# Scores of two slots in one visit, x^T between the double slots, PSUM laid out anew: threshold attention and an exact-Gelu MLP on one core

## The chip, the core and the metric

The kernel runs on one core of a Trainium2 chip. Its time is the device time of one execution in microseconds. Five engines work side by side and wait for each other by semaphores: TensorE (PE in the profile, its weight loads PEld), VectorE (DVE), ScalarE (ACT), GpSimd (POOL) and SyncE (SP, here only a queue of DMA issues). Each takes its instructions in the order in which the program was built.

## What is computed

```python
q, k, v: (8, 8, 576, 64)          # batch, heads, sequence, head dimension
scores = (q @ k^T) / 8
thresh = max(scores, -1) - tau
scores = where(scores >= thresh, scores, -1e9)
attn = exp(scores - max(scores));  attn /= sum(attn) + 1e-9
x = (attn @ v) laid out as (8*576, 512)
h = x @ w_in                       # (512, 2048)
out = (0.5 * h * (1 + erf(h / sqrt(2)))) @ w_out
```

All of it is float32. On TensorE a float32 matmul of this kernel is two instructions.

## The kernel before

**Pairs and slots.** Two heads of a batch make a pair; there are 32 pairs (`NP`), four to a batch. The 576 rows of a pair's scores are four chunks of 128 rows per head and a tail of 64 rows; the two tails share one tile. So a pair has five slots (`SLOTS`): chunks 0 to 3, each with both heads (`e` = 0, 1), and the tail (`NC` = 4). The first four pairs (`EARLY`) run in another way, with transposes on TensorE; the change leaves them nearly alone. From the fifth pair on the loop at line 1060 treats one slot after the other.

**A slot.** `scores` (L394) multiplies 64 rows of q^T with k^T; the two heads use the two halves of the array's rows at the same time, in two matmuls of 288 columns each. Each head has a PSUM tile of two banks (tag `sc`, two buffers). `softmax_head` (L406) takes for each head the maximum on VectorE (L415), the threshold on GpSimd (L416), and the exponential on ScalarE (L418). `softmax_tail` (L421) reads the scores again on VectorE, multiplies the exponentials with (score >= threshold) and sums them (L434). After it the `sc` tile is free. `turn_p` (L488) transposes 32x32 blocks on VectorE into `turned_p` (chunks) or `pd_tail` (tail). `regroup` (L504) issues DMAs on SP that bring the turned blocks into `pT`, of which there is one per head; so they wait until x^T of the pair before has been computed. `weigh_v` (L522) multiplies v with `pT` to x^T, in two column spans of 320 and 256, each in a PSUM bank of the ring `mm`; ScalarE copies them to `xall` (L547). `divisors` (L466) sends the sums through DRAM, and `divide` (L556) scales x on GpSimd. `turn_qk` (L375) and `scale_q` (L371) prepare the next pair's q and k, which `load_steps` (L251) has fetched through GpSimd's queue.

**The MLP between the slots.** `fill` (L637) issues MLP matmuls into TensorE's order, so many after each slot as its share of a goal (`GOAL`, L1042) and of the five slots (`PARTS`, L1053) asks for. `block_steps` (L602) walks a block of 256 tokens: 16 groups of four matmuls of 256 columns into `hT` (one bank takes two groups, eight matmuls), then 2 x 16 matmuls of 512 columns into `o_ps`. The Gelu of an hT tile is an instruction of ScalarE (L586); `gelus(left)` (L573) issues those that wait until only `left` are left. They are issued after a slot's exponentials (L1075, with 0 left) or by `fill` when a further tile is complete and more than `lag` wait (`lag` = 2, L1133). Gelu and Exp need different tables of ScalarE, so a load stands ahead of each change; `table` (L596) brings the Exp table back. Eight blocks (`PLAIN`) are done so during attention; the other ten come after it in `last_blocks` (L973), with fewer products by a Strassen scheme.

**PSUM.** One pool `ps` (L80) for the whole kernel: ring `mm` of four banks (hT, o_ps, x^T, transposes) and ring `sc` of two tiles of two banks, eight banks in all.

**Order before in a pair**, on TensorE: scores of chunk 0, fill, chunk 1, fill, chunk 2, x^T of the pair before (`WEIGH` = 2), a short fill, chunk 3, fill, tail, fill.

Of the kernel before, what the change touches and what calls it, by code (L numbers as in the profile page):

```python
# [18 lines left out]
def kernel(  # L19
# [28 lines left out]
    nc = tc.nc  # L48
# [30 lines left out]
    dram = ctx.enter_context(tc.tile_pool(name="dram", bufs=1, space=bass.MemoryType.DRAM))  # L79
    ps = ctx.enter_context(tc.tile_pool(name="ps", bufs=4, space=PSUM))  # L80

# [62 lines left out]
    nc.vector.memset(zeros, 0.0)  # L144
    idle = ps.tile([P, 2 * P], FP32, tag="mm", name="idle")
    for _ in range(3):
# [154 lines left out]
    def turn_qk_early(p):  # L301
# [12 lines left out]
        for name in "qk":  # L314
            t = s[name]
            tr = ps.tile([P, NC, P], FP32, tag="mm", name="tr")
            for c in range(NC):
                for e in range(2):
                    nc.tensor.matmul(tr[e * D:(e + 1) * D, c, :], lhsT=t[:, e, c, :], rhs=ident, start=True, stop=True)
            src = tr.rearrange("p c s -> p (c s)")  # L320
            if name == "q":
                nc.scalar.activation(qT, src, AF.Copy, bias=0.0, scale=q_scale)
            else:
                copy(kT[:, TAIL:S], src)
        tr = ps.tile([P, NC, P], FP32, tag="mm", name="tr")
        for j, name in enumerate("qk"):
# [12 lines left out]
    def turn_p_early(p, i):  # L339
# [11 lines left out]
        for e in range(n):  # L351
            tr = ps.tile([P, NC, P], FP32, tag="mm", name="tr")
            for c in range(NC):
                turn(tr[:, c, :], e * (S + TAIL) + c * P)
            if i < NC:
                nc.scalar.copy(s["pT"][e][:, 0:NC, i * P:(i + 1) * P], tr)  # L356
# [4 lines left out]
        tails = s["pT"][0][:, NC, :]  # L361
        tr = ps.tile([P, NC, P], FP32, tag="mm", name="tr")
        turn(tr[:, 0, :], MAIN if i < NC else S - P)
# [29 lines left out]

    def scores(p, i):  # L394
        s = st[p]
        n = 1 if i == NC else 2
        sc = s["sc", i] = [ps.tile([P, 2, 512], FP32, tag="sc", name="sc", bufs=2) for _ in range(n)]
        for h in range(2):
            for e in range(n):
                rows = slice(0, P) if i == NC else slice(e * D, (e + 1) * D)  # L400
                lhsT = s["q_tail"] if i == NC else s["qT"][rows, i * P:(i + 1) * P]
                at = h * HALF + (TAIL if p < EARLY and e == 0 else 0)
                nc.tensor.matmul(  # L403
                    sc[e][:, h, 0:HALF], lhsT=lhsT, rhs=s["kT"][rows, at:at + HALF], start=True, stop=True)

    def softmax_head(p, i):  # L406
# [6 lines left out]
        for e in range(n):  # L413
            sc = s["sc", i][e][:, :, 0:HALF]
            nc.vector.tensor_reduce(nmx[:, e:e + 1], sc, axis=AXIS.XY, op=ALU.max, negate=True)  # L415
            nc.gpsimd.tensor_scalar(  # L416
                thr[:, e:e + 1], nmx[:, e:e + 1], -1.0, tau_eff, op0=ALU.mult, op1=ALU.subtract)
            nc.scalar.activation(  # L418
                w[:, e * S:(e + 1) * S].rearrange("p (h s) -> p h s", h=2), sc, AF.Exp, bias=nmx[:, e:e + 1], scale=1.0)

    def softmax_tail(p, i):  # L421
# [10 lines left out]
        for e in range(n):  # L432
            row = w[:, e * S:(e + 1) * S].rearrange("p (h s) -> p h s", h=2)
            nc.vector.scalar_tensor_tensor(  # L434
                row, sc[e][:, :, 0:HALF], thr[:, e:e + 1], row, op0=ALU.is_ge, op1=ALU.mult, accum_out=den[e])
        if p < EARLY:
# [8 lines left out]
    def divide_early(p, lo, hi):  # L445
# [3 lines left out]
        b, hp = divmod(p, HP)  # L449
        tr = ps.tile([P, 512], FP32, tag="mm", name="tr")  # L450
        for i in range(lo // P, -(-hi // P)):
# [69 lines left out]

    def weigh_v(p, lo, hi):  # L522


        b, hp = divmod(p, HP)
        s = st[p]
        xT = ps.tile([P, 512], FP32, tag="mm", name="xT")
        for c in range(KR):
            for e in range(2):
                f = slice(e * D, (e + 1) * D)  # L530
                to = xT[f, 0:hi - lo]
                if p < EARLY:
                    rhs = s["pT"][0 if c == NC else e][:, c, lo:hi]
                else:
                    to = to.rearrange("p (g s) -> p g s", s=2 * Q)
                    rhs = by_64(s["pT"][e])[:, lo // (2 * Q):hi // (2 * Q), c, :]
                nc.tensor.matmul(  # L537
                    to, lhsT=s["v"][:, e, c, :], rhs=rhs, start=(c == 0), stop=(c == KR - 1))
        for n, o, at, size in in_blocks(b, lo, hi):
            if n not in x_blk:  # L540
# [61 lines left out]
    def block_steps(n):  # L602
# [3 lines left out]
        for j in range(N_DF):  # L606
            if j % 2 == 0:
                hT = None
            for c in range(N_DM):
                yield NS_IN, (j * P // PIECE + 1) * N_DM  # L610
                if hT is None:
                    hT = ps.tile([P, 2, TOK], FP32, tag="mm", name="hT")
                nc.tensor.matmul(hT[:, j % 2, :], lhsT=w_in_sb[c][:, j * P:(j + 1) * P], rhs=x_blk[n][:, c, :],  # L613
                                 start=(c == 0), stop=(c == N_DM - 1))
            if j % 2:
                late.append((g, j, hT))
                gelus(lag[0])
        x_free.append(x_at.pop(n))
        for m in range(TOK // P):
            for j in range(N_DF):  # L620
# [5 lines left out]
                if j == 0:  # L626
                    o = ps.tile([P, 512], FP32, tag="mm", name="o_ps")
                nc.tensor.matmul(o[:, 0:d_model], lhsT=g[j][:, m * P:(m + 1) * P], rhs=w_out_sb[j],  # L628
                                 start=(j == 0), stop=(j == N_DF - 1))
            o_sb = op.tile([P, d_model], FP32, tag="o_sb", name="o_sb")  # L630
            nc.scalar.copy(o_sb, o[:, 0:d_model])
            row = n * TOK + m * P
            nc.sync.dma_start(out[row:row + P, :], o_sb)

    mlp = {"n": 0, "steps": None, "next": None, "debt": 0.0, "layer": 0}

    def fill(ns, tokens):  # L637

        mlp["debt"] += ns
        while True:  # L640
# [7 lines left out]
            took, need = mlp["next"]  # L648
            if mlp["debt"] <= 0 or need > converted[0]:
                break  # L650
# [153 lines left out]
    def bank(tag, n):  # L804
        if tag == "sc":
            return ps.tile([P, 2, 512], FP32, tag="sc", name="bank", bufs=2)[:, 0, 0:n]
        return ps.tile([P, 512], FP32, tag="mm", name="bank")[:, 0:n]

# [221 lines left out]

    parts = [(range(2), HP), (range(2, SLOTS), HP)] + [(range(SLOTS), 1)] * (NP - HP)
    slots = []
# [19 lines left out]

    PARTS = 1.3, 1.3, 0.2, 1.3, 0.9  # L1053

# [5 lines left out]
    for n in range(len(slots) + WEIGH + 1):  # L1060
        p, i = slots[n] if n < len(slots) else divmod(n, SLOTS)
        early = p < EARLY
        last = slots[n - 1] if 0 < n <= len(slots) else None
        if p < NP:
            scores(p, i)
            softmax_head(p, i)
            add_low_bits()
# [4 lines left out]
        elif n == len(slots):  # L1072
            early_end.close()
            weights_first()
        gelus(0)  # L1075
        if n == BATCH:
            gelus_held()
        table()
        for args in due:
            weigh_v(*args)  # L1080
            divide_early(*args)
        due = []
        if p > EARLY and i == WEIGH:
            for lo, hi in (0, WIDE), (WIDE, S):
                weigh_v(p - 1, lo, hi)
            if p == NP:
                divide(p - 1)
        owed += (goal(n) - goal(n - 1)) * BLK_NS * (PARTS[i] if not early and p < NP else 1.0)
        if early:
# [7 lines left out]
        if p < NP:  # L1097
            softmax_tail(p, i)
        if p < NP and not early:
            turn_p(p, i)  # L1100
        if p < NP and not early:
            if i == 2:
                regroup(p, 1)
            if i > 2:
                regroup(p, i)
            if i == NC:
                divisors(p)
# [10 lines left out]
        if n == BATCH:  # L1118
            for t in pd_tail + [turned_p[:, e, h, :, :] for e in range(2) for h in range(2)]:
                nc.gpsimd.memset(t[:, NB:4 * KR, :], 0.0)  # L1120
        if EARLY < p < NP and i == DIVIDE:
            divide(p - 1)
        if p >= HP and i == 1 and p + 2 < NP:
            loads = load_steps(p + 2)
        if p >= HP:
            next(loads, None)
        if p >= HP and i == 1 and p + 1 < NP or p == HP - 1 and i == 2:
            scale_q(p + 1)
        if p >= HP - 1 and i == 2 and p + 1 < NP:
            turn_qk(p + 1)  # L1130
        convert(0 if n == 0 else 1200 if n < 3 else 2200 if n < BATCH - 1 else 1e9)
        if not early:
            lag[0] = 2 if p < NP else 0  # L1133
            if n != BATCH:
                fill(owed, tokens)
                owed = 0.0
# [7 lines left out]
        elif n == BATCH + 1:  # L1144
            tokens = S
        elif p > EARLY and i == DIVIDE and p % HP == 0 or p == NP and i == WEIGH:
            tokens = p // HP * S
            leaving += [n for n in AWAY if n in x_blk and (n + 1) * TOK <= tokens]
        elif leaving and i < 2:
            put_away(leaving.pop(0))  # L1150
    fill(1e12, B * S)
    late_end.close()
    last_blocks()

# [31 lines left out]
```

## Time and profile before

| | us |
|---|---|
| median of 3 runs (1350.87 to 1352.63) | 1350.93 |
| the profiled execution | 1353.51 |
| its span, first to last instruction | 1351.4 |
| mean of an exponential (L418), 288 of them | 0.738 |
| mean of a maximum (L415) | 0.750 |
| mean of a threshold step (L434) | 0.816 |
| mean of a chunk's turn (L498) | 1.378 |
| mean of a Gelu (L586), 56 of them | 0.597 |
| one table load of ScalarE, 55 at L586 and 55 at L599 | 1.283 |

How to read it: the page gives each engine's busy time, then the span in 40 slices, then the chain of work that ended last, then groups of instructions of one line, with the mean of one and the idle time just before them. The early pairs take the first 190 us or so, attention with MLP between runs to about 860 us, and the last ten blocks take the rest. In a stretch of the attention stage the maxima, thresholds, turns and exponentials of one pair (some 25 us) are all there, and the busy shares say how near each engine is to being the bound.

### The profile page before, as it was taken

How to read it: one execution, taken by the hardware profiler on the slowest of the kernel's cores; microseconds unless marked ns; L12 is line 12 of the kernel's file. 1: busy time of each engine (PE TensorE's matmuls, PEld its weight loads, DVE VectorE, ACT ScalarE, POOL GpSimd, SP SyncE). 2: the span in 40 equal slices, each digit the busy share in tenths (PEclk: the TensorE clock that was granted, in tenths of full speed). 3: DMA queues.
4: the chain of work that ended last, by engine and by line, in shares of the span. 5: the costliest groups of instructions: out<-in, count | busy, mean ns of one | idle time of the engine just before them, and what ended most of it. 6: DMA issues, size and time to landing. Idle time of an engine off the chain costs nothing.

```text
span 1351.4 us, 19821 instructions
## 1 busy us (share of the span) xinstructions
PE 1323.0 (98%) x6282; PEld 893.8 (66%) x6282; DVE 1048.1 (78%) x1997; ACT 605.0 (45%) x1027; POOL 659.0 (49%) x1097
## 2 busy tenths in 40 slices
PE   8799899999999999999999999999999999999998
PEld 6476557467467557557557557568787787877877
DVE  6987677788888888888888888874758698385765
ACT  7876527548547538537638636413201112211120
POOL 5785354555555554554554551144363513635530
PEclk9899999999999999999999999999999999999999
DMA  8642276677777787687687777500000041000003
GB/s 268 187 151 52 58 164 156 146 162 185 155 180 182 161 193 178 160 207 172 153 208 180 155 179 152 117 9 0 1 0 1 14 112 32 0 1 0 1 0 78
DMA packets 209781, 152.39 MB, mean 113 GB/s; under 512 B 113360, under 2 KB 193088, under 8 KB 209680
## 3 DMA queue, kind: packets, MB, share of 16 engines
q1 hardware_dynamic: 188224, 112.53, 37.5%
q0 software_dynamic: 21024, 38.32, 9.9%
q8 instruction: 51, 0.84, 0.3%
q14 instruction: 50, 0.41, 0.1%
q10 hardware_dynamic: 432, 0.30, 0.1%
HBM read 55.97 MB, written 12.52 MB: 51 GB/s over the span
## 4 chain that ended last, share of the span: by engine, by line
PE 93%; DVE 3%; ACT 3%; DMA 1%; issue 1%; SPq 0%; POOL 0%; DVEq 0%; ACTq 0%; POOLq 0%
PE bank L801 34%; PE o_ps L628 17%; PE hT L613 16%; PE sc L403 14%; PE xT L537 11%; ACT p L418 1%; DMA x<-xall 1%; DVE nmx L415 1%; DVE p L434 1%; PE tr L349 1%; ACT pT L356 1%; DVE power L212 0%; ACT power L202 0%; DVE power L210 0%; PE tr L456 0%
## 5 line engine op out<-in xcount | busy, mean ns | idle before, releaser
L418 ACT ACTIVATE p<-sc,nmx 128x576 f32<-128x576 f32 x288 | 201.9, 738 | 284.0 <-DVE nmx L415 283.7
L434 DVE SCALAR_TENSOR_TENSOR p<-sc,thr,p 128x576 f32<-128x576 f32 x288 | 225.3, 816 | 70.1 <-ACT p L418 68.6
L416 POOL TENSOR_SCALAR thr<-nmx,tau_eff 128x1 f32<-128x1 f32 x288 | 88.0, 307 | 368.0 <-DVE nmx L415 355.8
L415 DVE TENSOR_REDUCE nmx<-sc 128x1 f32<-128x576 f32 x288 | 205.4, 750 | 53.5 <-PE sc L403 52.3
L613 PE MATMUL hT<-xall,w_in 128*128 128x256 f32 x1024 | 241.8, 385 | 0.0
L628 PE MATMUL o_ps<-w_out,g 128*128 128x512 f32 x512 | 236.8, 603 | 0.0
L613 PEld LDWEIGHTS hT<-xall,w_in 128*128 128x128 f32 x1024 | 189.4, 190 | 50.0 <-issue 23.0
L683 DVE TENSOR_TENSOR c<-c,bank 128x320 f32<-128x320 f32 x304 | 147.3, 488 | 33.6 <-PE bank L801 20.1
L683 DVE TENSOR_TENSOR o<-o,bank 128x256 f32<-128x256 f32 x240 | 99.8, 420 | 93.7 <-PE bank L801 88.7
L403 PE MATMUL sc<-kT,qT 64*128 64x288 f32 x960 | 161.8, 431 | 9.3 <-DVE p L434 8.6
L537 PE MATMUL xT<-pT,v 128*64 128x256 f32 (+1 forms) x1280 | 169.3, 418 | 0.8 <-DVE pT L360 0.5
L628 PEld LDWEIGHTS o_ps<-w_out,g 128*128 128x128 f32 x512 | 93.1, 190 | 109.1 <-issue 106.8
L498 DVE STREAM_TRANSPOSE turned_p<-p 128x1152 f32<-128x1152 f32 x112 | 154.4, 1378 | 3.9
L403 PEld LDWEIGHTS sc<-kT,qT 64*128 64x128 f32 x960 | 92.4, 187 | 83.8 <-issue 69.7
L537 PEld LDWEIGHTS xT<-pT,v 128*64 128x64 f32 x1280 | 93.0, 140 | 75.4 <-issue 15.1
L801 PE MATMUL bank<-w_out,c 128*128 128x256 f32 x480 | 120.2, 381 | 0.5 <-DVE o L683 0.5
L269 POOL DMA_DIRECT2D v<-in_v_dram x208 | 110.9, 536 | 3.9 <-issue 1.9
L801 PEld LDWEIGHTS bank<-w_out,c 128*128 128x128 f32 x480 | 89.9, 190 | 18.8 <-DVE o L683 3.0
L854 ACT ACTIVATE c<-c 128x320 f32<-128x320 f32 (+1 forms) x80 | 46.9, 623 | 114.6 <-DVE c L683 114.6
L683 POOL TENSOR_TENSOR c<-c,g 128x320 f32<-128x320 f32 (+1 forms) x40 | 50.5, 1271 | 67.4 <-DVE c L683 67.4
L801 PE MATMUL bank<-t_out,c 128*128 128x256 f32 x320 | 82.7, 381 | 0.0
L801 PE MATMUL bank<-t_out,g 128*128 128x256 f32 x320 | 82.1, 379 | 0.0
(179 smaller groups left out, 1775.1 us busy)
## 6 DMA issues: line engine op xcount, KB each, us to landing
pT<-turned_p SPq DMA_DIRECT2D x448, 160.0 KB, 3.6
pT<-pd_tail SPq DMA_DIRECT2D x112, 80.0 KB, 3.0
q<-in_q_dram POOLq DMA_DIRECT2D x104, 72.0 KB, 3.4
k<-in_k_dram POOLq DMA_DIRECT2D x104, 72.0 KB, 3.2
inv<-turned SPq DMA_DIRECT2D x54, 128.0 KB, 3.9
v<-in_v_dram POOLq DMA_DIRECT2D x156, 40.0 KB, 3.1
out_dram<-o SPq DMA_DIRECT2D x40, 128.0 KB, 2.4
xall<-in_moe_w_out_dram POOLq DMA_DIRECT2D x9, 512.0 KB, 3.8
```

Of the source, the lines that this page charges most:

```text
L269: eng.dma_start(t[r:P:4, e, 0:n, :], rows[:, r * KR:r * KR + n, :])
L403: nc.tensor.matmul(sc[e][:, h, 0:HALF], lhsT=lhsT, rhs=s["kT"][rows, at:at + HALF], start=True, stop=True)
L415: nc.vector.tensor_reduce(nmx[:, e:e + 1], sc, axis=AXIS.XY, op=ALU.max, negate=True)
L416: nc.gpsimd.tensor_scalar(thr[:, e:e + 1], nmx[:, e:e + 1], -1.0, tau_eff, op0=ALU.mult, op1=ALU.subtract)
L418: nc.scalar.activation(w[:, e * S:(e + 1) * S].rearrange("p (h s) -> p h s", h=2), sc, AF.Exp, bias=nmx[:, e:e + 1], scale=1.0)
L434: nc.vector.scalar_tensor_tensor(row, sc[e][:, :, 0:HALF], thr[:, e:e + 1], row, op0=ALU.is_ge, op1=ALU.mult, accum_out=den[e])
L498: nc.vector.transpose(turned_p[:, :, i // 2, 0:NB, i % 2 * Q:(i % 2 + 1) * Q], w.rearrange("p (e b i) -> p e b i", e=2, i=Q))
L537: nc.tensor.matmul(to, lhsT=s["v"][:, e, c, :], rhs=rhs, start=(c == 0), stop=(c == KR - 1))
L613: nc.tensor.matmul(hT[:, j % 2, :], lhsT=w_in_sb[c][:, j * P:(j + 1) * P], rhs=x_blk[n][:, c, :], start=(c == 0), stop=(c == N_DM - 1))
L628: nc.tensor.matmul(o[:, 0:d_model], lhsT=g[j][:, m * P:(m + 1) * P], rhs=w_out_sb[j], start=(j == 0), stop=(j == N_DF - 1))
L683: eng.tensor_tensor(out, a, b, op=ALU.add)
L801: nc.tensor.matmul(to, lhsT=l, rhs=r, start=start and k == 0, stop=k == len(pairs) - 1, skip_group_check=not start)
```

## The change

From the third slot of the fifth pair on (`JOIN` = BATCH + 2):

- PSUM is laid out anew: ring `mm` has two banks, ring `sc` two tiles of three banks. For this the pool is closed and opened again, at `JOIN` and ahead of the last blocks, and the MLP tile that is open at `JOIN` is finished first.
- A pair's slots are visited in the order chunk 0, chunk 1, tail, chunk 2, chunk 3. At chunk 0 and at chunk 2 the scores of two chunks are made in one visit: a head has one tile of three banks, each bank takes 192 columns of the first chunk and 192 of the second. So a chunk's scores are three matmuls of 192 columns per head in place of two of 288. Both chunks' maxima and exponentials follow, then both chunks' threshold steps. At chunk 1 and chunk 3 there is only the rest (turn, fill, regroup).
- x^T of the pair before is made at the tail slot, both spans in one tile of the ring `sc`.
- `regroup` of chunks 0 and 1 and of the tail is issued at the tail slot, that of chunks 2 and 3 at the last slot, where `divisors` follows it.
- `lag` is 1 in place of 2, `PARTS` has other shares, and Gelus and the table are taken up only where scores are made.

```diff
-    ps = ctx.enter_context(tc.tile_pool(name="ps", bufs=4, space=PSUM))
+    banks = ctx.enter_context(ExitStack())
+    space = {}
+
+    def lay_out_banks(name, mm, width):
+        banks.close()
+        space["pool"] = banks.enter_context(tc.tile_pool(name=name, bufs=mm, space=PSUM, reuse_waits="tile"))
+        space["width"] = width
+
+    def psum(shape, name, tag="mm"):
+        return space["pool"].tile(shape, FP32, tag=tag, name=name)
+
+    def score_banks(name):
+        return space["pool"].tile([P, space["width"], 512], FP32, tag="sc", name=name, bufs=2)
+
+    lay_out_banks("ps", 4, 2)
...
-    def scores(p, i):
+    def scores(p, i, both=False):
...
+        units = [i, i + 1] if both else [i]
+        wide = S // 3 if both else HALF
+        sc = [score_banks("sc") for _ in range(n)]
+        for k, c in enumerate(units):
+            s["sc", c] = [t[:, 0:S // wide, k * wide:(k + 1) * wide] for t in sc]
+            for h in range(S // wide):
+                for e in range(n):
...
+                    at = h * wide + (TAIL if p < EARLY and e == 0 else 0)
+                    nc.tensor.matmul(
+                        s["sc", c][e][:, h, :], lhsT=lhsT, rhs=s["kT"][rows, at:at + wide], start=True, stop=True)
...
-            if mlp["debt"] <= 0 or need > converted[0]:
+            if not (close and mlp["open"]) and mlp["debt"] <= 0 or need > converted[0]:
...
-    parts = [(range(2), HP), (range(2, SLOTS), HP)] + [(range(SLOTS), 1)] * (NP - HP)
+    parts = [(range(2), HP), (range(2, SLOTS), HP)] + [((0, 1, NC, 2, 3), 1)] * (NP - HP)
...
-    PARTS = 1.3, 1.3, 0.2, 1.3, 0.9
+    PARTS = 1.2, 1.2, 0.4, 1.1, 1.1
+    JOIN = BATCH + 2
...
+        pos = n % SLOTS
+        if n == JOIN:
+            gelus(0)
+            lay_out_banks("ps_joined", 2, 3)
+        single = n < JOIN or i == NC
         if p < NP:
-            scores(p, i)
-            softmax_head(p, i)
+            if single:
+                scores(p, i)
+                softmax_head(p, i)
+            elif i % 2 == 0:
+                scores(p, i, both=True)
+                softmax_head(p, i)
+                softmax_head(p, i + 1)
...
-        gelus(0)
-        if n == BATCH:
-            gelus_held()
-        table()
+        if p == NP or single or i % 2 == 0:
+            gelus(0)
+            if n == BATCH:
+                gelus_held()
+            table()
...
-        if p > EARLY and i == WEIGH:
-            for lo, hi in (0, WIDE), (WIDE, S):
-                weigh_v(p - 1, lo, hi)
+        if p > EARLY and pos == WEIGH:
+            xT = score_banks("xT")
+            weigh_v(p - 1, [(0, WIDE), (WIDE, S)], [xT[:, half, :] for half in range(2)])
...
-            softmax_tail(p, i)
+            if single:
+                softmax_tail(p, i)
+            elif i % 2 == 0:
+                softmax_tail(p, i)
+                softmax_tail(p, i + 1)
...
-            if i == 2:
+            if pos == 2:
                 regroup(p, 1)
-            if i > 2:
-                regroup(p, i)
-            if i == NC:
+                regroup(p, NC)
+            if pos == 4:
+                regroup(p, 3)
                 divisors(p)
...
-            lag[0] = 2 if p < NP else 0
+            lag[0] = 1 if p < NP else 0
             if n != BATCH:
-                fill(owed, tokens)
+                fill(owed, tokens, n == JOIN - 1)
...
     late_end.close()
+    lay_out_banks("ps_last", 4, 2)
     last_blocks()
```

## The prediction

> **What bounds the kernel now.** I read the summary and the chain that ended last, then busy time in stretches of 100 us, then the waits inside the attention stage, and then the time line of one slot.
>
> ```profile
> PE 1323.0 (98%) x6282; PEld 893.8 (66%) x6282; DVE 1048.1 (78%) x1997; ACT 605.0 (45%) x1027; POOL 659.0 (49%) x1097
> ...
> PE 93%; DVE 3%; ACT 3%; DMA 1%; issue 1%; SPq 0%; POOL 0%; DVEq 0%; ACTq 0%; POOLq 0%
> ...
> 500.00:600.00 100.00, 100.00 (x493) 59.71 (x490) 87.20 (x157) 58.45 (x90) 55.08 (x112) 1.00 0.77 180
> ```
>
> TensorE holds 93% of the last chain, and in a stretch of the attention stage it is never idle while VectorE is at 87%. So a microsecond of TensorE work saved there is a microsecond of time, and so is one that TensorE waits.
>
> ```profile
> PE sc L403 <- DVE p L434: 1.6, 2, 1.3
> ...
> DVE p L434 <- ACT p L418: 58.0, 128, 2.5
> DVE nmx L415 <- PE sc L403: 30.8, 55, 1.1
> ```
>
> In the waits from 200 to 850 us TensorE waits 1.6 us in all; VectorE (from 180 to 840) waits 58.0 us for exponentials and 30.8 us for scores. With four `mm` banks no hT tile waits for its bank.
>
> ```profile
> 508.99 3.72 PE L613 MATMUL hT<-xall,w_in 128*128 128x256 f32 x16
> 509.00 1.42 DVE L415 TENSOR_REDUCE nmx<-sc 128x1 f32<-128x576 f32 x2
> ...
> 510.11 1.35 ACT L418 ACTIVATE p<-sc,nmx 128x576 f32<-128x576 f32 x2
> 510.93 0.82 DVE L434 SCALAR_TENSOR_TENSOR p<-sc,thr,p 128x576 f32<-128x576 f32 x1 [0.51 <-ACT p L418]
> 511.48 1.28 ACT L586 ACT_TABLE_LOAD   x1
> ...
> 512.64 1.24 PE L403 MATMUL sc<-kT,qT 64*128 64x288 f32 x8
> 512.77 0.60 ACT L586 ACTIVATE g<-hT 128x512 f32<-128x512 f32 x1
> 513.39 1.28 ACT L599 ACT_TABLE_LOAD   x1
> 513.81 1.35 PE L613 MATMUL hT<-xall,w_in 128*128 128x256 f32 x5
> 513.91 1.42 DVE L415 TENSOR_REDUCE nmx<-sc 128x1 f32<-128x576 f32 x2
> ```
>
> One slot: scores, two maxima of 0.75 us, two exponentials of 0.74 us, two threshold steps; on ScalarE the Gelu stands behind the exponentials, with a table load of 1.28 us. An hT matmul is two instructions of 0.216 us ((3.72 - 0.38 tail - 0.1 start) / 15), so 0.43 us. Tail slots follow each other by 24.2 to 26.4 us in most pairs, 28 us in the first ones.
>
> **The skill.** (1) *TensorEngine Tiling (Array Packing)*, Key Properties: changing the tiling mode drains TensorE. The trace agrees: from the first hT to the first score there are 3.65 us (512.64 - 508.99) where 16 instructions need 3.45, and from the first score to the next hT 1.17 us where four concurrent pairs of 0.24 (288 columns, by 0.216 for 256) need 0.97. So a visit in 64-row mode costs 0.4 us beside its work. (2) *PSUM — Partial Sum Buffer*, PSUM bank collisions: two engines may not touch one bank at once, reads included. Accordingly the built order makes the second slot's maximum wait for the first slot's exponential of the same head; no run shows that wait yet. (3) *TensorE: Matmul & The Clock Gate*, Part 1: the clock halves after an idle window of some 3.4 us. The trace agrees in its early part (columns: PE, PEld, DVE, ACT, POOL busy, granted clock, DMA):
>
> ```profile
> 44.00:48.00 4.00, 0.77 (x8) 0.53 (x5) 3.96 (x9) 2.81 (x6) 3.47 (x7) 1.00 0.47 147
> 48.00:51.40 3.40, 3.29 (x10) 2.10 (x12) 3.37 (x6) 2.97 (x7) 3.19 (x5) 0.50 0.51 149
> 51.40:54.80 3.40, 3.40 (x18) 1.89 (x16) 3.40 (x10) 1.41 (x2) 2.35 (x5) 0.50 0.80 273
> ```
>
> A gap of 3.3 us is followed by 6.8 us at half clock, 3.4 us lost. In windows of 3.4 us laid from the clock's own steps, the busiest that was followed by half clock had 42% of work, the idlest that was not, 47%. (4) The same page, LDWEIGHTS: 128 columns take P/1.2 = 107 ns.
>
> **Part by part**, for the 28 pairs in the new layout.
>
> *Switches.* Before: three lone score visits (0.40 each) and scores, x^T, MLP in a row (three switches, 0.54): 1.74 us a pair. After: two double visits (0.8) and x^T alone beside the tail (whose scores use the full array, no switch): 0.35. Saved 0.59 a pair, 28 pairs: **-16.5 us**.
>
> *192 columns.* Six concurrent pairs of 2 x 0.163 = 1.95 us replace two visits of 0.97; no difference if the weight load (107 ns of occupancy by the skill) hides under 160 ns. Its row reads 187 ns in this trace; were that the pace, 24 instruction pairs x 25 ns x 28 = +17 us. I take 0, because 128-column transposes in the trace follow each other at 0.109 us, faster than their own loads of 141 ns.
>
> *The second mm bank pair goes.* This decides. With two `mm` banks an hT tile needs the Gelu of the tile two before it. In the built order that Gelu mostly stands on ScalarE behind the four exponentials of the double visit that TensorE has just left. From the end of the scores, by the rows above: max 0.75; exponential 0.88 to 1.62; the second slot's maximum waits for it, 1.72 to 2.47; its exponential 2.60 to 3.34; for the other head 0.67 later, 4.01; table load to 5.31; Gelu to 5.91; TensorE goes on at 6.0. In that time TensorE has only what stands before the tile. I went through all hT and o_ps tiles of the built order: 25 start behind such a Gelu after a double visit, with 169 hT matmuls between the visits and them (1 to 12 each, 6.8 on average). Waits: 25 x 6.0 - 169 x 0.431 = 77.2, plus 0.8 where a scaling of q stands in front. Ten visits hold a second such tile, behind Gelu, table load, 0.1, q scaling 0.76, table load and Gelu (10.05); eight matmuls after 6.0 TensorE is at 9.45: nine times 0.57, and 0.4 behind an output copy: 5.6. Sum **+83.7 us**. Behind the tail the same Gelu is ready at 3.6, under x^T (5.1 us): nothing. Bounds: 70 if the chain is 0.5 us shorter, 95 if as much longer.
>
> *Clock.* Twenty of these waits last 2.5 to 5.6 us. Idle of that length fills over half of a 3.4 us window in perhaps 7 of 10; each costs 1.7 (one window at half clock) or 3.4. At most 20 x 2.4 = 48; part falls under the next wait. I take half, **+24**; bounds 0 and 48.
>
> *Joining.* The o tile is finished first (16 o_ps matmuls run ahead), then tail and double visit stand back to back: the second score tile waits for the tail's threshold step (2.2), the next double visit for the thresholds behind it (3.5): **+5**, bounds 0 and 10.
>
> *o_ps pairs.* About nine pairs have no hT. TensorE has 23.6 us of work there, VectorE about as much as before, for 24.6. A double block keeps VectorE 9.3 us (thresholds done at 5.8 and 6.55, two turns after), while its next scores come a whole fill later; it then idles 0.5 to 0.8 us before the second double visit and comes 1.2 late to the next, so that the tail's bank is late by about 1. Such a pair stays near 24.6 to 25.2 instead of gaining 0.6: **+7**, bounds 0 and 14.
>
> *x^T in score banks.* All copies wait for its last matmul and take 1.0 us; the fill (0.86 to 1.3) and the switch (0.2) cover them. Without that cover 1 us a pair. *Regroup.* Twelve issues of 0.78 after x^T end 9.4 us later, before the last turn; then eight (6.2) and 3.6 to land: all there 19.1 us after the second double visit, x^T's second half needs them at about 19: covered where TensorE waits, at most 0.5 in o_ps pairs (in the bound above). SP's divisor transfers follow as before. POOL's thresholds stand behind four load issues of 0.69, done before the next scores. Fewer table switches on ScalarE are worth nothing, it is 58% busy.
>
> Sum: -16.5 + 83.7 + 24 + 5 + 7 = +103. The profiled execution took 1353.51 us (span 1351.4, 2.1 around it), 2.6 above the median of 1350.93; its sum is 1456.7, and against the median I say **1454 us**.
>
> **Rivals.** *Faster:* the Gelus come in time and only the switches count: 1351 - 16.5 = 1334. For it: TensorE is saturated and the drains are in the trace. Against it: the Gelu would have to end within the 0.4 to 5.2 us that TensorE still has, 2.9 on average, and four exponentials alone take 4.0; below 3.6 us (25 x 0.65 = 16 us of waits) this side wins. *VectorE takes over without Gelu waits:* pairs of 24.6 to 25.6 as before, 1345 to 1370. *Waits without a lower clock:* 1351 + 79 = 1430, with the chain shorter 1410. *Weight loads set the pace of 192 columns* too: 1471, up to 1495 with the full clock loss.
>
> **Numbers.** Forecast (1435 to 1475) 0.55; waits at full clock 0.22; above 1475 0.12; VectorE alone 0.06, of which 0.02 within 0.2%; faster 0.05. The range leaves out the last two and the far top: 1405 to 1490. A measurement can tell 0.2% from no change. Faster 0.05, same 0.02, slower 0.93.
>
> **What would show it.** Right: idle of TensorE before hT, put down to ACT g, some 80 us over the attention stage, longest near 5.6; tail slots 29 to 32 us apart in hT pairs, 24 to 25.5 in o_ps pairs; clock below 1.0 in stretches of the stage; score visits of about 2 us without such gaps inside. Wrong: hT tiles that start on time, or 192-column pairs 0.19 us apart, or a clock of 1.00 throughout.

## The result and the profile after

The changed kernel takes 1474.72 us (median of 4 runs, 1470.45 to 1477.91) against 1351.78 us for the kernel before: 1.0908 times as long, 95% interval 1.0876 to 1.0939. The forecast was 1454 us with a range of 1405 to 1490.

First the page of the changed kernel, its busy times, the chain that ended last and three groups (busy, mean ns of one, then idle time before them and what ended most of it):

```profile
span 1471.5 us, 20449 instructions
PE 1356.1 (92%) x6722; PEld 951.3 (65%) x6722; DVE 1032.4 (70%) x1997; ACT 611.6 (42%) x1014; POOL 662.3 (45%) x1097
...
PE 64%; DVE 11%; DMA 9%; ACT 8%; SPq 5%; issue 3%; POOL 0%; DVEq 0%; ACTq 0%; POOLq 0%
...
L437 DVE TENSOR_REDUCE nmx<-sc 128x1 f32<-128x576 f32 x288 | 205.0, 749 | 218.9 <-PE sc L422 210.6
L633 PE MATMUL hT<-xall,w_in 128*128 128x256 f32 x1024 | 271.0, 420 | 62.4 <-ACT g L605 61.9
...
L422 PE MATMUL sc<-kT,qT 64*128 64x192 f32 (+1 forms) x1400 | 153.5, 350 | 27.1 <-ACT xall L566 14.8
```

TensorE fell from 98% busy to 92% and from 93% of the last chain to 64%. What took its place is not one engine: VectorE, DMA, ScalarE and SP's queue share the rest. VectorE did not become the bound; it is 70% busy and now waits 210.6 us for scores. Two idle times of TensorE stand out in the groups, 61.9 us of hT behind `ACT g` (the Gelu) and 14.8 us of scores behind `ACT xall` (the copies of x^T).

The waits of TensorE from 180 to 1000 us (engine, line, what it waited for: us in total, times, longest):

```profile
PE hT L633 <- ACT g L605: 61.9, 23, 5.4
PE sc L422 <- ACT xall L566: 14.8, 3, 7.3
PE o_ps L650 <- ACT g L605: 6.1, 2, 3.2
PE xT L556 <- DMA pT<-turned_p: 1.1, 3, 0.4
PE sc L422 <- DVE p L455: 1.0, 3, 0.5
```

The kernel before had 1.6 us there. One of the 23 waits in its order of time, the longest:

```profile
679.48 2.22 PE L422 MATMUL sc<-kT,qT 64*128 64x192 f32 x24
...
681.63 0.70 PE L633 MATMUL hT<-xall,w_in 128*128 128x256 f32 x2
...
682.02 2.95 DVE L437 TENSOR_REDUCE nmx<-sc 128x1 f32<-128x576 f32 x4
682.77 1.41 ACT L440 ACTIVATE p<-sc,nmx 128x576 f32<-128x576 f32 x2 [6.25 <-DVE nmx L437]
684.33 1.41 ACT L440 ACTIVATE p<-sc,nmx 128x576 f32<-128x576 f32 x2 [0.16 <-DVE nmx L437]
685.76 1.28 ACT L605 ACT_TABLE_LOAD   x1
...
687.05 0.60 ACT L605 ACTIVATE g<-hT 128x512 f32<-128x512 f32 x1
...
687.70 2.93 PE L633 MATMUL hT<-xall,w_in 128*128 128x256 f32 x6 [5.38 <-ACT g L605]
```

The scores end at 681.70 (679.48 + 2.22). TensorE adds one matmul (two instructions) to an open tile and then needs a bank for the next. Its Gelu stands behind four exponentials (the two pairs of 1.41 us) and a table load, though the hT tile it reads was complete before the scores began. TensorE goes on 6.0 us after the scores, the value that the prediction had worked out from the rows of the kernel before. VectorE starts 0.3 us after the scores here; after 17 of the 24 double visits that such a wait follows, worked out from the starts of the matmuls, TensorE goes on after 5.76 us.

The same stretch in windows as long as the clock's own steps (us from the start; length, then PE, PEld, DVE, ACT, POOL busy with the number of instructions, granted clock, DMA share, GB/s):

```profile
679.97:683.38 3.41, 2.36 (x24) 1.73 (x20) 3.34 (x7) 0.61 (x1) 2.29 (x5) 1.00 0.44 81
683.38:686.79 3.41, 0.00 (x0) 0.00 (x0) 3.06 (x8) 3.23 (x5) 2.31 (x6) 1.00 0.95 190
686.79:690.20 3.41, 2.50 (x6) 2.05 (x7) 3.41 (x6) 3.35 (x6) 1.24 (x2) 0.50 0.98 236
690.20:693.61 3.41, 3.41 (x10) 2.69 (x9) 0.56 (x1) 2.81 (x3) 0.00 (x0) 0.50 0.27 33
693.61:697.02 3.41, 3.41 (x17) 2.95 (x16) 0.00 (x0) 0.00 (x0) 0.00 (x0) 1.00 0.36 91
```

The window without TensorE work is followed by two at half clock; the second of these holds 10 instructions of TensorE in the same busy time in which the window behind it, at full clock, holds 17. From 190 us on there are 18 such episodes, nine of 3.4 us and nine of 6.8, 92 us in all. By the distances of the matmuls in them, 44 us are lost (half of the time in which TensorE is recorded as busy there would be 40).

The other wait, with the copies of x^T and SP's transfers beside it:

```profile
659.90 0.32 ACT L566 COPY xall<-xT 128x192 f32<-128x192 f32 x1 [2.32 <-PE xT L556]
...
660.63 1.07 SPq L689 DMA_DIRECT2D x<-xall  x2
...
661.28 0.59 PE L422 MATMUL sc<-kT,qT 64*128 64x192 f32 x2
...
667.56 0.43 ACT L566 COPY xall<-xT 128x128 f32<-128x128 f32 x2 [7.35 <-DMA x<-xall]
668.81 0.27 ACT L566 COPY xall<-xT 128x128 f32<-128x128 f32 x1 [0.81 <-DMA x<-xall]
...
669.13 4.17 PE L422 MATMUL sc<-kT,qT 64*128 64x192 f32 x22 [7.27 <-ACT xall L566]
```

A copy of x^T needs a place in `xall` that is free only when `put_away` has carried an older block to DRAM. SP issues these two transfers from 660.63 on, after the divisors' own; the copies that wait for them go on at 667.56 and 668.81. x^T now lies in a tile of the ring `sc`, and after the first head's first matmul (two instructions, into the other tile) the scores wait for it. ScalarE's copies waited for these transfers in the kernel before too, in the same stretch of 180 to 1000 us:

```profile
ACT xall L547 <- DMA x<-xall: 14.4, 4, 5.1
```

There x^T lay in `mm` banks and TensorE had others.

### The profile page after: what moved, and what is told of

The parts are those of the page before. It is cut to its first block, busy times and chain, and to the rows that moved or that the text cites. A ratio compares the mean times of both kernels' runs of the same rounds, so it can differ in the third digit from the quotient of the medians.

```text
span 1471.5 us, 20449 instructions
## 1 busy us (share of the span) xinstructions
PE 1356.1 (92%) x6722; PEld 951.3 (65%) x6722; DVE 1032.4 (70%) x1997; ACT 611.6 (42%) x1014; POOL 662.3 (45%) x1097
## 4 chain that ended last, share of the span: by engine, by line
PE 64%; DVE 11%; DMA 9%; ACT 8%; SPq 5%; issue 3%; POOL 0%; DVEq 0%; ACTq 0%; POOLq 0%
PE bank L824 31%; PE hT L633 9%; PE xT L556 8%; PE o_ps L650 7%; PE sc L422 7%; DMA pT<-turned_p 4%; DVE nmx L437 4%; ACT p L440 4%; SPq L541 4%; DVE p L455 3%; DVE turned_p L519 3%; DMA turned<-turned 3%; ACT L605 2%; DMA x<-xall 1%; ACT g L605 1%
## 5 line engine op out<-in xcount | busy, mean ns | idle before, releaser
L437 DVE TENSOR_REDUCE nmx<-sc 128x1 f32<-128x576 f32 x288 | 205.0, 749 | 218.9 <-PE sc L422 210.6
L633 PE MATMUL hT<-xall,w_in 128*128 128x256 f32 x1024 | 271.0, 420 | 62.4 <-ACT g L605 61.9
L633 PEld LDWEIGHTS hT<-xall,w_in 128*128 128x128 f32 x1024 | 208.9, 210 | 119.8 <-ACT g L605 71.5
L455 DVE SCALAR_TENSOR_TENSOR p<-sc,thr,p 128x576 f32<-128x576 f32 x288 | 220.9, 815 | 44.5 <-ACT p L440 43.4
L422 PE MATMUL sc<-kT,qT 64*128 64x192 f32 (+1 forms) x1400 | 153.5, 350 | 27.1 <-ACT xall L566 14.8
L422 PEld LDWEIGHTS sc<-kT,qT 64*128 64x128 f32 x1400 | 126.6, 195 | 63.9 <-issue 44.5
L519 DVE STREAM_TRANSPOSE turned_p<-p 128x1152 f32<-128x1152 f32 x112 | 147.6, 1356 | 0.1
```

What stands on the lines that cost most here:

```text
L422: nc.tensor.matmul(s["sc", c][e][:, h, :], lhsT=lhsT, rhs=s["kT"][rows, at:at + wide], start=True, stop=True)
L455: nc.vector.scalar_tensor_tensor(row, sc[e], thr[:, e:e + 1], row, op0=ALU.is_ge, op1=ALU.mult, accum_out=den[e])
L519: nc.vector.transpose(turned_p[:, :, i // 2, 0:NB, i % 2 * Q:(i % 2 + 1) * Q], w.rearrange("p (e b i) -> p e b i", e=2, i=Q))
```

## The experiments

All are the changed kernel with the edit shown; times are medians, ratios stand against runs of the kernel before taken beside them (1352.6 to 1353.8 us). "Waits" are TensorE's from 180 to 1000 us. "Half clock" is the recorded time at half clock from 190 to 1010 us.

**The Gelus first.** What is ready for its Gelu is taken up ahead of the scores and their exponentials:

```diff
+        if n >= JOIN and p < NP and (single or i % 2 == 0):
+            gelus(0)
+            table()
```

> The changed kernel with one edit: from the joined stage on, the Gelus that are due and the return of the Exp table are issued ahead of a visit's scores and exponentials, not behind them. Theory (an hT tile waits for a Gelu that stands behind the visit's exponentials): TensorE's waits for ACT g fall from 72 us to about 10 (tiles that start 8 or more matmuls after a visit still need a Gelu of the same fill), the half clock in the stage from 92 us to under 35, the time from 1475 to 1355 to 1385. Rival (two mm banks and two table loads per Gelu are too little for ScalarE wherever the Gelu stands, or the exponentials now come late): waits of over 40 us for ACT g or as much for DVE stay, time above 1430.

Measured: 1394.35 us, ratio 1.0311 [1.0293, 1.0328]; 80 us of the 123 are gone. Half clock fell from 92 to 24 us. The waits:

```profile
PE hT L633 <- ACT g L605: 14.1, 11, 3.0
PE sc L422 <- ACT xall L566: 12.5, 3, 5.5
PE o_ps L650 <- ACT g L605: 3.5, 3, 3.0
```

So the order on ScalarE is what TensorE waited for: the number of banks is the same, and only the place of the Gelus, with their table loads, differs. 50 us of waits and, at half speed, some 30 us of clock went together. The time lies 9 us above what was expected: eleven waits for hT and three for o_ps stay, for tiles whose last matmul comes after the scores.

**The put-away transfers on another queue.**

```diff
-        nc.sync.dma_start(away[n], x_blk.pop(n))
+        nc.gpsimd.dma_start(away[n], x_blk.pop(n))
```

> The changed kernel with one edit: the five x blocks that are put away to DRAM are issued on GpSimd's queue in place of SP's. Theory (three score visits wait 15 us in all for x^T copies, because the copies wait for these transfers, which SP issues only after regroup and divisors): the wait of sc for ACT xall falls from 15 us to under 4, the time by 15 to 22 us to 1453 to 1460, clock included. Rival (the transfer itself is long, or x^T is late for another reason): wait stays over 10 us, time within 5 us of the changed kernel's 1475.

Measured: 1463.26 us, ratio 1.0809 [1.0783, 1.0835], 11 us less; this is 3 us above the range of the theory and outside that of its rival. The wait for `ACT xall` is gone and those for the Gelu are as before. Part of the gain is given back: x^T now waits 6.7 us for the transfers of p, in the changed kernel 1.1:

```profile
PE hT L633 <- ACT g L605: 63.0, 23, 5.7
PE xT L556 <- DMA pT<-turned_p: 6.7, 5, 2.3
PE o_ps L650 <- ACT g L605: 6.1, 2, 3.1
PE sc L422 <- DVE p L455: 1.4, 5, 0.5
```

**A visit for every slot, two banks kept.** The order of the slots, x^T in the ring `sc` and two `mm` banks stay; no scores are made for two slots at once:

```diff
-        single = n < JOIN or i == NC
+        single = True
```

> The changed kernel with each chunk's scores in a visit of its own again (two matmuls of 288 columns, one exponential per head), the new slot order, two mm banks and x^T in score banks kept. Theory (ring of two behind a visit's exponentials; the waits scale with how many exponentials stand in front): a Gelu is then ready 4.2 us after a visit in place of 6.0; by the built order about 30 tiles wait, 1.2 to 3.8 us each, 55 to 65 us in all, seldom long enough to lower the clock (half clock under 45 us); switches cost 0.2 us a pair more than before; time 1415 to 1445. Rival (the double visit itself is the cost, its four exponentials in a row): waits under 20 us, time below 1375.

Measured: 1462.86 us, ratio 1.0815 [1.0795, 1.0835]; half clock 34 us.

```profile
PE hT L633 <- ACT g L605: 46.8, 23, 3.6
PE o_ps L650 <- ACT g L605: 7.9, 5, 3.0
PE sc L422 <- ACT xall L566: 5.6, 3, 3.1
```

The time is above the expected range. With two exponentials ahead of a Gelu instead of four the longest wait falls from 5.4 to 3.6 us (TensorE goes on 4.1 to 4.2 us after most visits, where 4.2 was expected), but they stay about as many. So the double visit makes the waits longer; it is not what makes them. That the half clock fell further (to 37%) than the waits (to 80%) fits a clock that falls only after a mostly idle window.

**The same with four banks.** Score tiles of two banks leave room for four `mm` banks; against the last kernel only their number differs:

```diff
-            lay_out_banks("ps_joined", 2, 3)
-        single = n < JOIN or i == NC
+            lay_out_banks("ps_joined", 4, 2)
+        single = True
```

> The kernel after with a visit for every slot and with score tiles of two banks, so that four mm banks remain; tail slot in the middle, x^T in score banks beside it and the new order of the slots stay. Against e3 it differs in the number of mm banks alone. Theory (the ring of two mm banks is the whole of the Gelu waits, and the half clock follows from them): no wait of TensorE for ACT g above 3 us in sum, half clock under 10 us in the stage, and the time is that of the kernel before plus 28 x 0.2 us of one more switch a pair and some 6 us of score visits behind the x^T copies: 1355 to 1370 us. Rival (the new place of the tail slot and of x^T costs by itself, on VectorE's chain or through the put-away transfers): 1385 to 1440 us with the waits for ACT g gone.

Measured: 1396.48 us, ratio 1.0315 [1.0292, 1.0337]; half clock 10 us. In TensorE's waits one line is left, and VectorE waits for scores 83.6 us (33.6 in the kernel before, same stretch). The waits of TensorE:

```profile
PE sc L422 <- ACT xall L566: 8.0, 3, 3.4
```

Those of VectorE:

```profile
DVE nmx L437 <- PE sc L422: 83.6, 54, 6.1
```

The theory holds for the waits: with four banks there is no wait for a Gelu, and the time is 66 us below that of the single visits with two banks, where 54.7 us of waits and about 12 us of lost clock ((34 - 10) / 2) had stood. But the time is in the rival's range: in single visits the rest of the change costs 43 us by itself. With the order of the slots come x^T in the ring `sc`, a `lag` of 1, other shares of the fill and other places of `regroup`, and no run separates these. From the start of the first to that of the last matmul of a score visit, worked out from the trace (mean ns; the four visits in their order after the tail, which ends a pair in the kernel before and stands in the middle here):

```
kernel before          1082   846   847   838
this kernel            1402   982  1159  1202
```

That is 1.13 us a pair, 31 us over 27 pairs, with the waits for `ACT xall` in it. Most of the last two visits of a pair (39 of 48) begin with an instruction alone: the next follows 0.30 us later on average instead of 0.007. In 36 of the 39 VectorE was then at a threshold step of the slot before, whose bank the second head's scores need; such waits are too short for the list. Drains, the time that TensorE loses when it changes its mode, explain 5.6 us more (four lone visits and the tail with x^T cost 4 x 1.369 + 6.169 us, before 3 x 1.369 + 6.369 + 0.970: 0.2 a pair), half clock and joining some 10.

**The first two together.**

> Both edits together: Gelus ahead of the scores, and x blocks put away on GpSimd's queue. Theory: what is left is the saved switches of 16 us against some 10 us of Gelu waits, a few us of half clock, the joining and the o_ps pairs: 1340 to 1365, waits for ACT xall under 4 us. If VectorE's chain of a pair is the next bound: hT pairs near 25 us, time 1350 to 1365; if not: pairs near 24.3, time below 1345.

Measured: 1382.55 us, ratio 1.0225 [1.021, 1.0241]: 12 us less than with the Gelus first alone, so the two effects add; above the expected range all the same. 19.5 us of Gelu waits stay, and 14 us of half clock.

**Fills that end with whole tiles.** The remaining Gelu waits are for tiles that a visit finds half done. Ahead of a double visit a begun hT tile is finished, and at most two tiles are begun between two score visits; the Gelus come first as above. In one kernel `put_away` is on POOL, with the edit shown above; in another it is on SP but issued where the block is set aside, by the last two lines, which stand in this one alone:

```diff
-            if not (close and mlp["open"]) and mlp["debt"] <= 0 or need > converted[0]:
+            shut = close and mlp["open"] or whole and mlp["whole"]
+            if not shut and mlp["debt"] <= 0 or need > converted[0]:
+                break
+            if not mlp["open"] and mlp["tiles"] >= mlp["most"]:
                 break
...
+            gelus(0)
+            table()
+            mlp["tiles"], mlp["most"] = int(mlp["open"]), 2
...
-                fill(owed, tokens, n == JOIN - 1)
+                fill(owed, tokens, n == JOIN - 1, n >= JOIN and p < NP and pos in (1, 4))
...
+            while n > JOIN and p < NP and leaving:
+                put_away(leaving.pop(0))
```

> Both edits of e4, and the fills of the joined stage cut at hT tiles: a fill ahead of a score visit ends with a complete hT tile, and at most two tiles are begun between two score visits; so no tile in the built order stands behind a Gelu of its own visit. Theory (what e4 still pays is 21 us of waits for Gelus of the same fill, some 10 us of half clock with them, and 8 us of x^T waiting for its transfers): waits for ACT g under 3 us, half clock under 10 us, time 1348 to 1360. Rival (the fills' distribution was right, and cutting it starves VectorE, so that score visits wait for banks): DVE waits of TensorE over 15 us and a time of 1370 or more.

> As e5_whole_tiles_pool, but the x blocks are put away on SP's queue again, issued at the slot of the division, ahead of the last regroup, in place of GpSimd's queue one pair later. Theory (on GpSimd's queue the put-away transfers run beside the last regroup's, and x^T waits for those; at the earlier place they run in a free stretch): waits of xT for the pT transfers fall from 7 us to under 3, waits of sc for ACT xall stay under 4, time 1338 to 1350, so faster than the kernel before by 0.2 to 1%. Rival (x^T's waits come from the regroup issues themselves, 0.78 us each): they stay at 6 us or more and the time equals e5_whole_tiles_pool within 3 us.

Measured: 1366.49 us with POOL (ratio 1.0095 [1.0082, 1.0108]) and 1365.20 us with the early issue on SP (1.0081 [1.0063, 1.01]). No wait for a Gelu is left with two banks. Of the second kernel:

```profile
PE sc L422 <- DVE p L455: 7.2, 14, 1.2
PE xT L556 <- DMA pT<-turned_p: 3.6, 5, 1.1
PE xT L556 <- DMA q<-in_q_dram: 1.7, 2, 0.9
PE sc L422 <- ACT xall L566: 1.7, 4, 0.4
```

The place of `put_away` makes no difference that these runs can tell (1.3 us), which is what its rival said of the time; that the second kernel would gain ten more was wrong. x^T's waits for the transfers of p did fall, from 6.5 to 3.6 us, though the rival had them stay. The second kernel still stands 12 us above the kernel before although 16 us of drains are saved. Small waits take most of these 28 us: the 14.2 us shown, for VectorE, for transfers and for the copies, then 6 us at the joining and 3.4 us of lost clock behind it. That the rest lies in short gaps before weight loads is likely and not shown.

**The joining elsewhere.** `JOIN = BATCH + 3`, after the tail slot, and `JOIN = BATCH`, at the start of a pair:

> e5_whole_tiles_early with the joining one slot later, after the tail slot, so that the o tile that is finished ahead stands between the tail and the first double visit. In e5_whole_tiles_early TensorE waits some 6 us at the joining (0.7 + 2.1 + 3.0) and the clock falls to half for about 7 us behind it, 3.5 lost. Theory (the joining's back-to-back visits are what is left there): waits for VectorE at the joining fall to about 2.5 us and the half clock goes, 1357 to 1362 us. Rival (VectorE's own chain sets the slots by then, whatever TensorE saves): within 3 us of e5_whole_tiles_early.

> e5_whole_tiles_early with the joining at the beginning of the first pair of its own, two slots earlier, where no MLP tile is open. Theory: the first double visit follows a lone slot and no o tile has to be run ahead, so that at most 3 us of waits are left at the joining: 1356 to 1362 us. Rival: the MLP has then no tile to fill the first double visit's thresholds and the joining costs as much as before: 1362 to 1370 us.

Measured: 1360.28 us (1.0057 [1.0038, 1.0077]) and 1361.62 us (1.0061 [1.0044, 1.0077]), both within the range of the theory, 4 to 5 us less. (Their intervals overlap that of the kernel they start from, so this gain is likely, not certain.) The waits of TensorE for VectorE from 150 to 190 us, with the joining as it was:

```profile
PE sc L422 <- DVE p L455: 5.3, 3, 3.0
```

and in the later place:

```profile
PE sc L422 <- DVE p L455: 3.4, 2, 3.2
```

The wait fell by 1.9 us where about 2.8 were expected, and one window of half clock of the two went, 1.7 us; so the reason given is shown in part. With the start of a pair it is not shown. The time is just inside the range, but x^T waits 7.7 us there behind `DVE pT`, with 10.2 us at half clock, where at most 3 us of waits had been expected.

**The shares of the fill.** On top of the later joining, `PARTS = 1.1, 1.1, 0.4, 1.2, 1.2`, and `1.2, 1.2, 0.2, 1.2, 1.2`:

> e6_whole_tiles_join_later with the MLP work of a pair shared differently: 1.1, 1.1, 0.4, 1.2, 1.2 in place of 1.2, 1.2, 0.4, 1.1, 1.1, so that more of it stands between the second double visit and the first of the next pair, where TensorE's scores still wait for VectorE's threshold steps (7.2 us over the stage in e5_whole_tiles_early). Theory (these waits come from where the fill stands): the waits for VectorE halve and the time falls to 1353 to 1357 us. Rival (whole hT tiles of 6.9 us set the places, a tenth more or less moves few of them): within 3 us of 1360.

> The same with 1.2, 1.2, 0.2, 1.2, 1.2: half of the tail's own fill goes to the second double visit instead. Theory: waits for VectorE halve, while the copies of x^T stand bare behind the shorter fill and cost up to 0.5 us a pair: 1355 to 1368 us. Rival: within 3 us of 1360, as whole tiles set the places.

Measured: 1356.42 us (1.0037 [1.0023, 1.0051]) and 1356.38 us (1.0031 [1.0018, 1.0043]). Both are in the range of the theory, less than a microsecond outside the rival's (within 3 us of 1360). From 190 us on the waits for VectorE fell from 7.2 us (with the old shares) to 4.9 and 2.5, so that they halved in the second kernel alone; there those for the copies of x^T rose from 1.7 to 4.5 us. The double visit at a pair's start mostly no longer begins with a lone instruction (a median of 0.238 us between its first two with the old shares, 0.007 now). In the second kernel the waits are (from 130 us on, so with the joining):

```profile
PE sc L422 <- DVE p L455: 7.8, 9, 3.2
PE sc L422 <- ACT xall L566: 4.5, 11, 0.4
PE xT L556 <- DMA pT<-turned_p: 2.8, 4, 0.8
```

and its stage looks like that of the kernel before again, in the columns of the windows above:

```profile
200.00:300.00 100.00, 99.58 (x551) 66.08 (x549) 79.82 (x148) 50.65 (x81) 52.56 (x106) 1.00 0.74 157
500.00:600.00 100.00, 96.11 (x538) 63.20 (x534) 84.49 (x157) 47.24 (x76) 54.80 (x113) 1.00 0.83 182
700.00:800.00 100.00, 98.81 (x560) 66.55 (x558) 83.76 (x156) 50.90 (x81) 55.27 (x112) 1.00 0.83 175
```

This is the best of the new layout and still some 4 us above the kernel before. No version that was run beats it.

## Why the prediction was right, and where its sizes were off

The profiled spans differ by 120.1 us (1471.5 - 1351.4); the terms of the sum, as they were put and as measured in the trace after:

| term | predicted | measured |
|---|---|---|
| switches | -16.5 | -16.3 |
| Gelu waits | +83.7 | +72 |
| clock | +24 | +44 |
| joining | +5 | +5 |
| o_ps pairs | +7 | about 0 |
| x^T copies in the ring `sc` | 0 | +15 |
| sum | +103 | +120 |

- **Switches: right.** A double visit takes 2.348 us between the MLP matmuls around it, tail and x^T 6.169. Before, a chunk's visit took 1.369, the one with x^T 6.369, the tail 0.970. A pair: 3 x 1.369 + 6.369 + 0.970 = 11.446 against 2 x 2.348 + 6.169 = 10.865, 0.58 us less, times 28.
- **192 columns: right.** Concurrent pairs follow each other by 0.163 us (7 and 156 ns between starts); weight loads, though recorded with 0.195 us each, don't set the pace. The rival of 1471 to 1495 us hit the time by another way.
- **Gelu waits: right in mechanism, somewhat large.** 25 double visits with such a wait were predicted, ten of them with a second one; there are 24 and one (23 hT, two o_ps), up to 5.5 us, 72 us in all by the distance of the matmuls. The chain of mostly 5.76 us in place of 6.0 makes some 6 us of the 12 too many, the missing second waits 5. With the Gelus ahead of the exponentials most of it went (1394 us), with four banks all of it. The Trainium skill, *PSUM — Partial Sum Buffer*, PSUM bank collisions, keeps two engines off one bank at a time, reads included, so the built order makes the second slot's maxima wait for the first's exponentials. This showed no price: four maxima run in 2.95 us without a gap, as an exponential of the same head (0.74) ends while the other head's maximum (0.75) runs.
- **Clock: the term that was too small.** It was priced as half of 20 x 2.4. Each episode has the size predicted, 92 / 18 / 2 = 2.6 us, but there are 18 where ten were taken; three of them follow the waits behind x^T's copies, 15 the Gelus. The Trainium skill, *TensorE: Matmul & The Clock Gate*, Part 1, has the idle window of some 3.4 us; the trace agrees (683.38 to 686.79 above), and adds that a partly idle one is enough. In the changed kernel, from 190 us on, the busiest window that was followed by half clock was 42% busy (1.43 of 3.41 us, from 840.40 on), the idlest that was not 46% (1.58 us, from 229.40 on). This is no sharp limit: with single visits and two banks a window 42% busy (from 328.20 on) was not followed by half clock, and one 50% busy (from 713.90 on) was. The rival with waits at full clock (1430) is excluded by the recorded clock.
- **x^T in score banks: the step that failed, a term put at nothing.** It was said that the fill and the switch cover the copies. That holds for the copies' own 1.0 us; it misses that a copy may wait for a place in `xall`, thus for `put_away` on SP. The kernel before showed this very wait on ScalarE (14.4 us, four times, up to 5.1), where it cost nothing; with x^T in the ring of the scores it stops TensorE, 15.3 us in three stalls. The put-away experiment removed the wait and gave 11 us in all, with 5.6 us more of waits for p's transfers and less time at half clock (82 us).
- **o_ps pairs: wrong.** In six of the seven pairs without hT tail slots are 24.2 to 24.8 us apart, as low as before or lower, not 24.6 to 25.2. (In pairs with hT they are 24.2 to 43.3 us apart, a far wider spread than the 29 to 32 that were to show the mechanism.) VectorE's coupling appeared only where the Gelu waits are gone: the whole-tile kernels wait for VectorE, and reach 1356 to 1366 us, the rival "VectorE takes over without Gelu waits" (1345 to 1370).

So slower was right for the reason given. That the time also lies in the narrower range of 1435 to 1475 us is partly luck: errors of opposite sign (12 + 7 too much, 20 + 15 too little) leave 16 of the 20.7 us between forecast and median.

The 16 us of drains are saved and yet no kernel shows them in its time: with the Gelu waits gone, small waits for VectorE, for p's transfers and for the copies, and the joining, take them back. That most of these come from the coupling of TensorE and VectorE through two score tiles is a reading; which of them would have to go for a gain was not settled.

## What to carry to other kernels

Before a ring of buffers is made shorter, ask not how long its consumer takes but what stands ahead of the consumer on its engine when the buffer is filled; here the Gelu takes 0.6 us, and by its place in the queue it ends some 6 us after the scores. When a wait is off the critical path only because its buffer has spares, moving it into a tighter ring puts it on the path: look for such waits on every engine that reads the moved tile. Where TensorE gets idle times of some 3 us, add the clock to the price: here 44 us beside 87 of waits.

## What the runs showed of the hardware

- In the changed kernel TensorE stood idle for 2 us or more 23 times between 190 and 1010 us. Behind 18 of these (2.1 to 7.3 us long) the clock was at half for 3.4 or 6.8 us, nine times each; behind five (2.1 to 3.4 us) it was not. An episode at half clock costs at most 1.7 or 3.4 us. With waits of at most 3.6 us and about as many of them the half-clock time was 34 us instead of 92.
- A pair of concurrent 64-row instructions of 192 columns takes 0.163 us, of 288 columns 0.243 (7 and 236 ns between starts), in proportion to the columns.
- With four banks and single visits, 49 of 72 score visits (the second to fourth of a pair) begin with an instruction alone, the next 0.28 to 0.30 us later on average. They took 1.23 to 1.29 us on average from their first to their last matmul, the others 0.84.
